# Three hand-written step lists of a fused recurrence and feed-forward kernel, replaced by three others

## The chip, the cores and the metric

One core of one Trainium2 chip. The metric is the device time of the whole program in microseconds: 584.02 us before, the median of three runs (581.95 to 585.95).

## The reference, cut to what matters

```
for t in range(S):                       # q, k, v, alpha: (4, 8, 768, 48)
    state = alpha[t][:, None] * state + outer(k[t], v[t])
    y[t] = q[t] @ state
x = y as (3072, 384)
h = x @ w_in                             # (384, 2048)
sp = max(h, 0) + log1p(exp(-abs(h)))     # softplus
out = (h * erf(sp)) @ w_out              # (2048, 384)
```

A gated linear recurrence over 768 positions in 32 streams, then a feed-forward layer over 3072 tokens. The weights come as 8-byte floats.

## The kernel before, in words

The recurrence is cut into 24 chunks, each of 64 positions of 16 streams (two batches). Two chunks give one block of 256 tokens for the feed-forward layer, so there are 12 blocks, numbered 0 to 11. The inner width 2048 is cut into four groups g, each group into two halves. Matrix products that need more precision than one pass are made of three: high times high, high times low, low times high.

All work is written as small steps, and three lists of step names give their order:

- `ld_n` loads a chunk (seven DMAs on SP's queue, L147 and L151; the buffers of alpha, k and q are single, so a load waits until the chunk before it has been read).
- `a1` to `a5` are the recurrence of a chunk. DVE: scan (L156), K (L169, L170, L175), Q (L178), masked scores (L203), state T (L253, L255), `x_lo` (L275). ACT: L164 to L166, `kn` (L191), `x_hi` (L274). PE: L187, L198, L226, L237. The second chunk's `a5` completes the x of a block.
- `wi_n` (12 of them) and `wo_n` (16) load one piece of a weight and split it in high and low: one DMA on SP's queue (L390), two operations on ACT (L396, L379), four on DVE (L398, L401, L404, L380). Group g of H needs wi_3g to wi_3g+2; O_g_half needs two pieces of wo. The staging tile of a wi comes from the pool of `hs`, that of a wo from the pool of `s`, and the work tile of both from the pool of `w`.
- `H_g_half` multiplies x by a half group of w_in (18 matmuls, L310) and copies it out on ACT (L315) into `hs`.
- `U_g` is a tanh on ACT (L321), `L1_g` two logarithms and an exponential on ACT (L326 to L328), `L2_g` two operations on DVE (L334, L335), `G_g` a gelu on ACT (L338), `Z_g` two operations on DVE (L342, L343).
- `O_g_half` splits a half group in high (`gh`: DVE L356 for O_0_0 and O_2_0, ACT L358 for the rest) and low (`gl`: DVE L359) and makes 12 matmuls (L367) into `acc`. `out` copies acc on ACT (L375) and stores it.
- `GELU` and `LN` load the table of functions on ACT (L115). U and G need the one, a2 and L1 the other, so a block passes U, LN, L1, GELU, G, Z, O.

A suffix @n means a block n further on, and numbers in the chunk steps count from the chunk that the list is given. Pools: 5 tiles for `s`, 7 for `hs`, 4 for `w`, two for `gh` and `gl`, two banks for `acc`, two for `ph`, one tile for `o`.

`START` runs once: it loads and splits the weights, and makes chunks 0 to 5, H to L2 of block 0 and six half groups of H of block 1. `ORDER` runs for i = 1 to 11: G to out of block i-1, the last two half groups of H, then U, L1 and L2 of block i, chunks 2i+4 and 2i+5, and six half groups of H of block i+1. `TAIL` runs once: G to out of block 11. The lists set priorities: the framework that builds the program takes, for each engine, the earliest step of the list whose inputs and buffers it reckons to be ready. Which order came out is read from the trace. A step whose block or chunk lies past the end is skipped.

Of the kernel before, what the change touches and what calls it, by code (L numbers as in the profile page):

```python
# [23 lines left out]
LNEXP, GELU = "natural_log_exp_and_others", "gelu_and_others"  # L24
# [2 lines left out]
START, ORDER, TAIL = (  # L27
    z.split()
    for z in (
# [10 lines left out]
    )  # L40
)

# [2 lines left out]
def gla_moe(ctx: ExitStack, tc: tile.TileContext, q, k, v, alpha, w_in, w_out, out):  # L45
# [10 lines left out]
    NBLK = NT // TB  # L56
# [30 lines left out]
    for i in range(NI):  # L87
        half = maskn[i * TC : (i + 1) * TC]
        nc.gpsimd.affine_select(
            out=half, in_=half, pattern=[[1, TC]], compare_op=ALU.is_ge, fill=0.0, base=0, channel_multiplier=-1  # L90
# [412 lines left out]
    def run(order, c0, b0):  # L503

        for step in order:
            name, _, rel = step.partition("@")
            name, *arg = name.split("_")
            arg = [int(z) for z in arg]
            if name == "wi":
                weight_in(*arg)  # L510
            elif name == "wo":
                weight_out(*arg)
            elif name[0] in "la":
                if c0 + arg[0] < len(chunks):
                    ch = chunks[c0 + arg[0]]
                    if name == "a5":
                        ch.a5(moes[ch.n // 2])
                    elif name == "a6":
                        pass
                    else:  # L520
                        getattr(ch, name)()
            elif name in TABLES:
                new_phase(TABLES[name])
            elif b0 + int(rel or 0) < NBLK:
                getattr(moes[b0 + int(rel or 0)], name)(*arg)

    run(START, 0, 0)
    for i in range(1, NBLK):
        run(ORDER, 2 * i + 4, i)
    run(TAIL, 2 * NBLK, NBLK - 1)  # L530

# [3 lines left out]
        out=top[:, 0:2], in_=flags.rearrange("p n two -> p two n"), op=ALU.max, axis=mybir.AxisListType.X  # L535
# [67 lines left out]
```

## Time and profile before

| | us |
|---|---|
| median of three runs | 584.02 |
| the profiled execution, its own time | 582.33 |
| its span, first to last instruction | 580.4 |
| PE busy in the span | 519.5 |
| DVE busy | 483.6 |
| ACT busy | 468.6 |

The mean granted clock of TensorE over the span is 0.969 of full. The profile gives busy times of the engines: PE multiplies, PEld loads its weights, DVE and ACT work elementwise, SP issues the DMAs. L-numbers are lines of the kernel before. In a timeline each row has a start, a duration, the engine, the line, what is written from what, and in brackets the idle time before it with what ended that time.

### The profile page before, as it was taken

How to read it: one execution, taken by the hardware profiler on the slowest of the kernel's cores; microseconds unless marked ns; L12 is line 12 of the kernel's file. 1: busy time of each engine (PE TensorE's matmuls, PEld its weight loads, DVE VectorE, ACT ScalarE, POOL GpSimd, SP SyncE). 2: the span in 40 equal slices, each digit the busy share in tenths (PEclk: the TensorE clock that was granted, in tenths of full speed). 3: DMA queues.
4: the chain of work that ended last, by engine and by line, in shares of the span. 5: the costliest groups of instructions: out<-in, count | busy, mean ns of one | idle time of the engine just before them, and what ended most of it. 6: DMA issues, size and time to landing. Idle time of an engine off the chain costs nothing.

```text
span 580.4 us, 16926 instructions
## 1 busy us (share of the span) xinstructions
PE 519.5 (90%) x7386; PEld 496.0 (85%) x7386; DVE 483.6 (83%) x688; ACT 468.6 (81%) x704; POOL 2.4 (0%) x16
## 2 busy tenths in 40 slices
PE   0588687499999999999999999999999999999584
PEld 0486686488989999999999999999999999999584
DVE  6779969999999979969789699699699698594970
ACT  4446799579999799699699798797896996989911
POOL 1000000000000000000000000000000000000000
PEclk9999799789999999999999999999999999999878
DMA  6575633522412222212202312221211100000000
GB/s 194 177 230 168 203 91 107 178 86 63 128 28 61 76 55 62 64 52 75 88 25 65 88 32 72 75 61 43 73 62 44 53 8 30 1 29 1 28 0 33
DMA packets 36370, 43.64 MB, mean 75 GB/s; under 512 B 21952, under 2 KB 25024, under 8 KB 36288
## 3 DMA queue, kind: packets, MB, share of 16 engines
q1 hardware_dynamic: 36288, 42.48, 24.3%
q8 instruction: 60, 0.98, 0.7%
q14 instruction: 22, 0.18, 0.1%
HBM read 37.75 MB, written 4.72 MB: 73 GB/s over the span
## 4 chain that ended last, share of the span: by engine, by line
PE 69%; DVE 15%; ACT 9%; issue 3%; DMA 2%; SPq 0%; ACTq 0%; DVEq 0%
PE acc L367 29%; PE ph L310 29%; PE py L226 4%; PE pS L198 3%; DVE wbuf L401 2%; DVE s L342 2%; ACT s L326 2%; PE pu L237 1%; PE pn L187 1%; DVE wbuf L404 1%; DVE A L156 1%; DVE t L334 1%; DVE w L335 1%; DVE hs L343 1%; ACT hs L315 1%
## 5 line engine op out<-in xcount | busy, mean ns | idle before, releaser
L310 PE MATMUL ph<-x_hi,wi_hi 128*128 128x256 f32 x576 | 166.9, 290 | 7.5 <-ACT wi_hi L379 4.8
L310 PE MATMUL ph<-x_lo,wi_hi 128*128 128x256 f32 x576 | 164.0, 285 | 0.0
L310 PE MATMUL ph<-x_hi,wi_lo 128*128 128x256 f32 x576 | 163.7, 285 | 0.3 <-DVE wi_lo L380 0.2
L367 PE MATMUL acc<-wo_hi,gh 128*128 128x384 f32 x384 | 133.2, 347 | 16.4 <-DVE gh L356 16.4
L367 PE MATMUL acc<-wo_hi,gl 128*128 128x384 f32 x384 | 131.4, 346 | 2.0 <-DVE gl L359 1.9
L367 PE MATMUL acc<-wo_lo,gh 128*128 128x384 f32 x384 | 131.0, 341 | 0.0
L310 PEld LDWEIGHTS ph<-x_hi,wi_hi 128*128 128x128 f32 x576 | 111.4, 194 | 10.1 <-ACT wi_hi L379 5.1
L359 DVE TENSOR_TENSOR gl<-hs,gh 128x512 fp32r<-128x512 f32 x96 | 64.9, 686 | 58.4 <-ACT gh L358 57.6
L310 PEld LDWEIGHTS ph<-x_hi,wi_lo 128*128 128x128 f32 x576 | 111.5, 194 | 1.0 <-DVE wi_lo L380 0.8
L310 PEld LDWEIGHTS ph<-x_lo,wi_hi 128*128 128x128 f32 x576 | 111.0, 193 | 0.5 <-DVE x_lo L275 0.3
L367 PEld LDWEIGHTS acc<-wo_hi,gh 128*128 128x128 f32 x384 | 73.8, 192 | 18.0 <-issue 8.7
L315 ACT ACTIVATE hs<-ph 128x512 f32<-128x512 f32 x96 | 56.3, 590 | 39.3 <-PE ph L310 38.1
L367 PEld LDWEIGHTS acc<-wo_hi,gl 128*128 128x128 f32 x384 | 72.7, 191 | 7.4 <-DVE gl L359 7.0
L367 PEld LDWEIGHTS acc<-wo_lo,gh 128*128 128x128 f32 x384 | 73.7, 192 | 0.0
L334 DVE TENSOR_TENSOR t<-s,w 128x1024 f32<-128x1024 f32 x48 | 58.5, 1218 | 1.9 <-ACT w L328 1.4
L335 DVE SCALAR_TENSOR_TENSOR w<-t,w 128x1024 f32<-128x1024 f32 x48 | 58.4, 1216 | 0.3
L358 ACT ACTIVATE gh<-hs 128x512 fp32r<-128x512 f32 x72 | 44.9, 625 | 16.3 <-PE acc L367 12.5
L343 DVE SCALAR_TENSOR_TENSOR hs<-s,hs 128x1024 f32<-128x1024 f32 x48 | 57.9, 1215 | 0.1
L342 DVE TENSOR_TENSOR s<-s,w 128x1024 f32<-128x1024 f32 x48 | 57.5, 1215 | 0.4 <-ACT s L338 0.4
L326 ACT ACTIVATE s<-s,fixed 128x1024 f32<-128x1024 f32 x48 | 54.6, 1141 | 0.0
L321 ACT ACTIVATE s<-hs 128x1024 f32<-128x1024 f32 x48 | 49.7, 1055 | 1.6 <-DVE wbuf L398 0.9
L328 ACT ACTIVATE w<-w 128x1024 f32<-128x1024 f32 x48 | 50.4, 1051 | 0.3
(62 smaller groups left out, 715.1 us busy)
## 6 DMA issues: line engine op xcount, KB each, us to landing
raw_v<-in_v_dram SPq DMA_DIRECT2D x24, 448.0 KB, 3.7
wst<-in_moe_w_in_dram SPq DMA_DIRECT2D x12, 512.0 KB, 5.7
wst<-in_moe_w_out_dram SPq DMA_DIRECT2D x16, 384.0 KB, 3.7
raw_a<-in_alpha_dram SPq DMA_DIRECT2D x48, 96.0 KB, 2.9
raw_k<-in_k_dram SPq DMA_DIRECT2D x48, 96.0 KB, 2.2
raw_q<-in_q_dram SPq DMA_DIRECT2D x48, 96.0 KB, 2.3
out_dram<-o SPq DMA_DIRECT2D x24, 192.0 KB, 1.9
```

The lines of the kernel that those rows point to most:

```text
L310: nc.tensor.matmul(out=o, lhsT=wt[:, kt, fs], rhs=xt[:, kt, :], start=n == 0, stop=n == 3 * KT - 1)
L315: nc.scalar.activation(self.hs[g][:, sl], ph, AF.Copy)
L321: tab(nc.scalar.activation(self.s[g], self.hs[g], AF.Tanh, scale=-0.5))
L326: tab(nc.scalar.activation(s, s, AF.Ln, scale=0.5 - 2.0**-24, bias=bhalf))
L328: tab(nc.scalar.activation(w, w, AF.Exp, scale=-1.0))
L334: nc.vector.tensor_tensor(out=t, in0=s, in1=w, op=ALU.mult)
L335: nc.vector.scalar_tensor_tensor(out=w, in0=t, scalar=2.0, in1=w, op0=ALU.add, op1=ALU.mult)
L342: nc.vector.tensor_tensor(out=s, in0=s, in1=w, op=ALU.mult)
L343: nc.vector.scalar_tensor_tensor(out=h, in0=s, scalar=RT2 / 2, in1=h, op0=ALU.subtract, op1=ALU.mult)
L358: nc.scalar.activation(ghf, gg, AF.Copy)
L359: nc.vector.tensor_tensor(out=gl.rearrange("p a t -> p (a t)"), in0=gg, in1=ghf.bitcast(F32), op=ALU.subtract)
L367: nc.tensor.matmul(out=self.acc[tt][:, :DM], lhsT=gt[:, u, ts], rhs=wt[:, f, :], start=f == 0 and n == 0, stop=f == NF - 1 and n == 2,)
```

## The change

The three lists are replaced, and the loop over `ORDER` is shortened by one pass at either end. The new `START` also holds what the first pass of `ORDER` had (G to out of block 0, the rest of block 1, chunks 6 and 7, six half groups of H of block 2). The new `ORDER` runs for i = 2 to 10. The new `TAIL` also holds what the last pass had (G to out of block 10, the rest of block 11). The number of steps of each kind, the instructions of a step and the tiles stay as they are, and the tables are loaded as often (26 times).

```diff
@@ -27,16 +27,21 @@
-        "wi_1 wi_3 ld_0 wi_0 a1_0 a2_0 a3_0 ld_1 a4_0 wi_2 wi_4 a1_1 a5_0 a2_1 a3_1 a4_1 ld_2 wi_6 a5_1 a1_2 "
-        "a2_2 wi_7 wi_5 H_0_0 H_0_1 a3_2 a4_2 H_1_0 ld_3 wo_0 H_1_1 a1_3 wi_8 a5_2 a2_3 GELU wi_10 a3_3 ld_4 "
-        "wi_9 H_2_0 wi_11 wo_1 H_2_1 a4_3 H_3_0 H_3_1 U_0 U_2 a5_3 wo_3 wo_2 U_1 U_3 a1_4 H_0_0@1 H_0_1@1 LN "
-        "wo_5 L1_0 a2_4 a3_4 H_1_0@1 H_1_1@1 wo_4 L1_1 ld_5 L1_2 H_2_0@1 L2_0 wo_7 L2_1 L1_3 L2_2 a1_5 a2_5 a3_5 "
-        "wo_15 L2_3 wo_10 a4_4 a5_4 wo_9 wo_8 wo_11 ld_6 H_2_1@1 a4_5 a5_5 wo_6 wo_14 wo_12 wo_13 ",
-        "GELU a1_0 G_0@-1 G_1@-1 Z_0@-1 H_3_0 G_2@-1 U_0 H_3_1 Z_1@-1 O_0_0@-1 U_2 O_0_1@-1 O_1_0@-1 G_3@-1 U_1 "
-        "Z_2@-1 O_2_1@-1 O_1_1@-1 U_3 LN Z_3@-1 O_2_0@-1 a2_0 L1_0 a3_0 L2_0 a4_0 H_0_0@1 ld_1 a5_0 a1_1 a2_1 "
-        "a3_1 O_3_0@-1 L1_1 H_1_0@1 ld_2 H_1_1@1 L2_1 L1_2 a4_1 O_3_1@-1 H_2_0@1 L1_3 L2_2 H_2_1@1 a5_1 H_0_1@1 "
-        "L2_3 out@-1 ",
-        "GELU G_0 Z_0 O_0_0 G_1 G_2 Z_1 G_3 O_1_1 O_0_1 Z_2 O_1_0 Z_3 O_2_0 O_2_1 O_3_0 O_3_1 out ",
+        "wi_1 wi_0 ld_0 wi_3 a1_0 a2_0 a3_0 ld_1 a4_0 wi_6 a1_1 wi_2 wi_7 a2_1 a5_0 a3_1 ld_2 a4_1 a1_2 wi_4 "
+        "wi_8 a2_2 a5_1 a3_2 wi_5 H_0_0 H_0_1 ld_3 H_1_0 a4_2 wo_0 H_1_1 a5_2 a1_3 wi_9 a2_3 a3_3 wi_10 H_2_0 "
+        "wi_11 H_2_1 wo_1 H_3_0 GELU H_3_1 U_0 a4_3 U_2 ld_4 wo_3 a5_3 a1_4 H_0_0@1 U_1 wo_2 wo_11 U_3 wo_4 "
+        "H_0_1@1 LN L1_0 a2_4 wo_5 a3_4 ld_5 L1_1 a4_4 L1_2 L2_0 L2_1 L2_2 wo_10 a1_5 wo_7 L1_3 H_2_0@1 a2_5 "
+        "H_1_0@1 wo_6 a5_4 H_2_1@1 a3_5 wo_9 L2_3 a4_5 wo_15 ld_6 H_1_1@1 wo_12 wo_14 GELU wo_13 a5_5 G_0 G_1 "
+        "Z_0 H_3_0@1 Z_1 a1_6 H_3_1@1 U_0@1 wo_8 O_0_0 G_2 U_3@1 O_0_1 U_2@1 G_3 Z_2 O_1_1 U_1@1 LN Z_3 O_1_0 "
+        "a2_6 O_2_1 a3_6 L1_0@1 H_0_0@2 L1_3@1 ld_7 L2_0@1 a4_6 a5_6 a1_7 a2_7 H_1_0@2 O_3_0 O_2_0 H_0_1@2 a3_7 "
+        "L2_3@1 a4_7 L1_2@1 H_2_0@2 O_3_1 H_1_1@2 L2_2@1 L1_1@1 out H_2_1@2 a5_7 L2_1@1 ld_8 ",
+        "GELU G_0@-1 G_3@-1 Z_0@-1 G_2@-1 Z_2@-1 G_1@-1 O_0_0@-1 H_3_0 H_3_1 U_2 O_0_1@-1 a1_0 Z_1@-1 U_0 "
+        "O_1_0@-1 U_1 U_3 H_1_0@1 LN Z_3@-1 O_2_0@-1 a2_0 a3_0 L1_0 O_1_1@-1 a4_0 ld_1 O_2_1@-1 H_0_0@1 L1_2 "
+        "a1_1 a5_0 H_2_0@1 a2_1 H_0_1@1 O_3_0@-1 a3_1 L2_2 a4_1 ld_2 L1_1 L1_3 O_3_1@-1 H_1_1@1 out@-1 L2_0 a5_1 "
+        "H_2_1@1 L2_3 L2_1 ",
+        "GELU H_3_0 G_0@-1 H_3_1 G_1@-1 G_2@-1 Z_2@-1 Z_0@-1 U_0 O_0_0@-1 G_3@-1 Z_1@-1 O_0_1@-1 U_2 O_2_1@-1 "
+        "U_1 U_3 LN O_1_0@-1 O_2_0@-1 O_1_1@-1 Z_3@-1 O_3_0@-1 L1_0 O_3_1@-1 L2_0 L1_1 L1_2 L1_3 L2_1 L2_3 GELU "
+        "G_0 L2_2 Z_0 O_0_0 G_2 G_3 O_0_1 G_1 Z_1 O_1_1 O_1_0 Z_2 Z_3 O_2_1 O_2_0 O_3_0 out@-1 O_3_1 out ",
@@ -525,7 +530,7 @@
     run(START, 0, 0)
-    for i in range(1, NBLK):
+    for i in range(2, NBLK - 1):
         run(ORDER, 2 * i + 4, i)
     run(TAIL, 2 * NBLK, NBLK - 1)
```

## Rows read from the trace of the kernel before

**Rows 1.** The page's part 1: busy time, share of the span, instructions.

```profile
PE 519.5 (90%) x7386; PEld 496.0 (85%) x7386; DVE 483.6 (83%) x688; ACT 468.6 (81%) x704; POOL 2.4 (0%) x16
```

**Rows 2.** Busy time of each engine by stage; the second number is the stage's length.

```profile
core 0: us, PE busy (x) PEld busy (x) DVE busy (x) ACT busy (x) POOL busy (x), PEclk, DMA share, GB/s
0.00:34.60 34.60, 12.48 (x328) 10.57 (x328) 24.74 (x43) 15.66 (x33) 2.41 (x16) 1.00 0.69 215
34.60:76.50 41.90, 34.70 (x557) 31.84 (x558) 36.48 (x72) 26.25 (x49) 0.00 (x0) 0.92 0.54 167
76.50:99.00 22.50, 17.40 (x305) 15.88 (x303) 18.24 (x30) 22.47 (x37) 0.00 (x0) 1.00 0.33 104
99.00:115.00 16.00, 8.29 (x214) 7.31 (x214) 15.94 (x29) 10.60 (x19) 0.00 (x0) 0.76 0.52 157
115.00:177.30 62.30, 60.01 (x710) 55.92 (x712) 61.21 (x93) 57.32 (x89) 0.00 (x0) 0.95 0.27 79
177.30:527.60 350.30, 350.30 (x5085) 339.82 (x5086) 297.94 (x392) 308.06 (x449) 0.00 (x0) 1.00 0.18 53
527.60:544.80 17.20, 17.20 (x100) 16.45 (x98) 10.61 (x13) 16.94 (x21) 0.00 (x0) 1.00 0.00 1
544.80:553.40 8.60, 0.06 (x2) 0.00 (x0) 8.20 (x10) 6.90 (x9) 0.00 (x0) 0.66 0.13 47
553.40:572.10 18.70, 18.62 (x95) 18.14 (x96) 10.23 (x13) 3.48 (x7) 0.00 (x0) 0.88 0.01 2
```

**Rows 3.** Chain that ended last: start, length, what; steady stage and end.

```profile
411.89 12.70 PE acc L367 x72
...
453.54 12.70 PE acc L367 x72
...
517.13 10.61 PE ph L310 x90
```

**Rows 4.** SP's queue in the first 45 us: issues of loads.

```profile
15.19 0.81 SPq L147 DMA_DIRECT2D raw_k<-in_k_dram  x2
...
17.44 0.91 SPq L390 DMA_DIRECT2D wst<-in_moe_w_in_dram  x2
...
28.01 1.40 SPq L390 DMA_DIRECT2D wst<-in_moe_w_in_dram  x3
```

**Rows 5.** Groups by line and shape: busy, mean ns, idle before.

```profile
L315 ACT ACTIVATE hs<-ph 128x512 f32<-128x512 f32 x96 | 56.3, 590 | 39.3 <-PE ph L310 38.1 <-DVE gl L359 1.0
...
L375 ACT ACTIVATE o<-acc 128x384 f32<-128x384 f32 x24 | 11.7, 488 | 8.1 <-DMA out_dram<-o 5.0 <-PE acc L367 3.2
...
L401 DVE SCALAR_TENSOR_TENSOR wbuf<-wbuf 128x384 int32<-128x384 int32 x16 | 8.8, 551 | 1.7 <-ACT wbuf L396 1.6
...
L401 DVE SCALAR_TENSOR_TENSOR wbuf<-wbuf 128x512 int32<-128x512 int32 x12 | 8.2, 687 | 1.5 <-ACT wbuf L396 1.2
...
L398 DVE TENSOR_SCALAR wbuf<-wst 128x384 int32<-128x384 int32 x16 | 5.6, 353 | 1.3 <-DMA wst<-in_moe_w_out_dram 1.3
```

**Rows 6.** DVE's timeline, first LN stage: a wo that came late.

```profile
80.40 0.56 DVE L401 SCALAR_TENSOR_TENSOR wbuf<-wbuf 128x384 int32<-128x384 int32 x1 [1.62 <-ACT wbuf L396]
```

**Rows 7.** DVE's timeline, 99 to 118 us: Z of block 0 and its first gl.

```profile
106.02 1.21 DVE L343 SCALAR_TENSOR_TENSOR hs<-s,hs 128x1024 f32<-128x1024 f32 x1
...
112.28 1.22 DVE L343 SCALAR_TENSOR_TENSOR hs<-s,hs 128x1024 f32<-128x1024 f32 x1
...
116.63 0.68 DVE L359 TENSOR_TENSOR gl<-hs,gh 128x512 fp32r<-128x512 f32 x1
```

**Rows 8.** DVE's timeline, steady stage: low parts of O_0_0 and O_0_1.

```profile
444.54 1.29 DVE L359 TENSOR_TENSOR gl<-hs,gh 128x512 fp32r<-128x512 f32 x2
```

**Rows 9.** DVE's timeline, after the last table load: Z of block 11.

```profile
548.19 2.51 DVE L342 TENSOR_TENSOR s<-s,w 128x1024 f32<-128x1024 f32 x2
550.62 2.35 DVE L343 SCALAR_TENSOR_TENSOR hs<-s,hs 128x1024 f32<-128x1024 f32 x2
552.89 0.42 DVE L356 CAST gh<-hs 128x512 fp32r<-128x512 f32 x1
```

## The prediction

> **What bounds the kernel now.** First read the busy times of the whole span: PE 90%, DVE 83%, ACT 81% [rows 1]. Such an average says little, since no instruction is added or taken away; what an order can change are the idle stretches of the engine that sets the pace. So next come the stages [rows 2]. From 177.3 to 527.6 us PE is busy for all of 350.3 us while DVE and ACT have a seventh of the time free: the middle is bound by PE. Before it, PE is not the bound. In 99 to 115 us it works 8.29 of 16 us, while DVE works 15.94; in 115 to 177.3 DVE works 61.21 of 62.3. In 76.5 to 99, the first LN stage, ACT is full (22.47 of 22.5). At the end PE stands still for 8.6 us (544.8 to 553.4), while DVE and ACT bring the last block through GELU, G and Z. The chain of waits says the same [rows 3]: in the middle it is matmuls alone, and one pass of the list lasts 453.54 - 411.89 = 41.65 us.
>
> So the time is a start, a middle that runs at PE's pace, and an end. Work that the start brings to PE earlier moves everything behind it. I make the sum on the profiled execution's own time of 582.33 us (its span and 1.9 us around it), which is 1.7 us below the median of 584.02.
>
> **The start.** All of DVE's work in the start (28 weight splits, the first chunks, L2 and Z) is the same after the change, and from 99 to 177.3 us DVE is full. So the start can only be shortened by filling DVE's idle time before that. It has 41.90 - 36.48 = 5.42 us in 34.6 to 76.5 and 22.50 - 18.24 = 4.26 us in 76.5 to 99 [rows 2], together 9.7 us. The earlier idle time, 34.6 - 24.74 = 9.9 us, is mostly the wait for the first loads and the first chunk's chain, which the new list starts with the same steps; I leave it alone.
>
> What can fill it is a weight that has landed. SP's queue is in order, and a chunk's load waits there until the chunk before has been read: k of chunk 1 goes out at 15.19, and the weights behind it only at 17.44; the next three leave at 28.01, behind chunk 2 [rows 4]. A moved ld takes its seven DMAs along, a moved weight one. Counted in the lists, the weights ahead of ld_2, ld_3 and ld_4 are 5, 8 and 11 in the old one and 6, 9 and 14 in the new. So one more weight is at hand from the start, three more by ld_4. Also, six pieces of wo are listed before the first LN, four in the old. In the LN stage a wo has one staging tile left (four of five `s` hold the block), and DVE waits for it, as in the 1.62 us at 80.40 [rows 6].
>
> A wo costs DVE 0.353 + 3 x 0.551 = 2.0 us, a wi some 0.4 + 3 x 0.687 = 2.5 us [rows 5]; DVE's two other operations of each are as long as L401. Two wo and one wi drawn into idle time are 4.0 + 2.5 = 6.5 us. Bounds: 0, if the waits for tiles and for ACT stay where they are; 9.7, if all idle time goes. On the bad side, the new list has two more wi ahead of a5_1, so the first H may come 2 x 2.5 = 5.0 us later; PE has 41.9 - 34.7 = 7.2 us idle just behind, which hides it. If that cover were gone, the start would be 5.0 us longer. I take -6.5 us, being two thirds of the way to the largest gain.
>
> Where it should show: Z_0 of block 0 is half done at 106.02, but other work holds the first low part until 116.63 [rows 7]; some four wo lie between, and two fewer would bring O_0_0 forward by about 4 us. What is late next is DVE itself, until PE has its backlog.
>
> **The middle.** Nine passes at PE's pace cost the same in any order so long as PE never waits: 0 us. The cover is this. In the old order PE ends H_3_1 of a block at 411.89 (where the O of the block before begins), and its first low parts stand from 444.54 + 0.7 = 445.2 on: a chain of 33.3 us through U, LN, four L1, GELU, G, Z. PE wants them at 453.54, so 8.3 us are spare [rows 3, 8]. In the new list O_0_0 of the block before stands ahead of H_3_0 and H_3_1. A half of O is 12.70 / 6 = 2.12 us and a half of H 10.61 / 5 = 2.12 us [rows 3], so the distance from H_3_1 to the next O_0_0 falls to 41.65 - 3 x 2.12 = 35.3 us, and the spare time to 2.0 us. As long as the chain stays at 33.3, the change costs nothing; below it is a rival.
>
> **The end.** After H_3_1 of block 11 PE has the eight halves of O of block 10 (17.2 us [rows 2]) and then waits for the chain. In both lists those halves stand behind H_3_1, so that wait stays. One thing moves: before, Z_0 and Z_1 run interleaved (two L342, two L343), and the first gh comes at 552.89 [rows 9]. The new list has L2_2, then Z_0 and O_0_0, then G_2. If Z_0 runs alone, two operations of 1.2 us go out of the way: -2.4 us. If L2_2 or another Z slips in, 0. On the bad side, out of block 10 stands behind most of the last block, and O_0_0 needs its acc; two copies of 0.49 us with the three gelus ahead of them (some 1.1 us each, an estimate: twice the 0.59 of a copy half as long [rows 5]) are about +4 us. I take half the gain, -1.2 us.
>
> The 96 matmuls of the last eight halves take 18.62 us against 8 x 2.12 = 17.0; the granted clock is 0.66 of full over the idle stretch, between the levels of 1.2 and 2.4 GHz, and 0.88 over the burst [rows 2]. The Trainium skill, "TensorE: Matmul & The Clock Gate", section "HAM oscillation — how this bites in real kernels", puts such a loss to the idle gap ahead of a burst, so that a shortened gap would not give it back. If the loss came instead from low parts that arrive late, it would go with the interleaving, and the sum would be 1.6 us lower, 573.0. The clock in the row speaks for the Trainium skill's reading, and the sum does not count the 1.6.
>
> **Sum.** 582.33 - 6.5 + 0 - 1.2 = 574.6; I say 575.
>
> **Rivals.**
> *More is won.* All 9.7 us go, the end gives 2.4, and PE's 62.3 - 60.0 = 2.3 us of idle time in the catching up as well: 582.3 - 14.4 = 568. For it: three more weights by ld_4. Against it: staging tiles limit how early a wo can be split.
>
> *Nothing that can be told.* The lists are only priorities. In the old list every wo stood ahead of Z_0, yet some four lay between its halves and the first low part [rows 7]: tiles, not the list, timed them. If tiles time them again, the start keeps its length, and the time is 580 to 584; I write 582. That is also what it would be if the order on the engines hardly changed.
>
> *Slower.* The middle loses its cover. Place: O_0_0 of each pass, PE waiting for gl. In the old LN stage ACT copies about one `hs`; the new list puts up to six H of the next block, and out, between LN and GELU. Five more copies at 0.59 and two of out at 0.49 [rows 5] are 3.9 us: 33.3 + 3.9 = 37.2 us against 35.3, so 1.9 us in each of nine passes, 17 us: 574.6 + 17 = 592. It decides from a chain of 35.3 us on, and makes the kernel slower by over 1% from 37.0 us. For it: ACT and DVE work in order, so a copy ahead of L1 holds it up. Against it: H's copies come as PE makes them, much of this ACT work lies in the idle time of either stage anyhow, and Z_0 now stands earlier than G_2.
>
> **Chances and range.** About 1% (5.8 us) is what a measurement of this kernel can tell from no change: faster means below 578.2, slower above 589.9. My forecast (571 to 578) 0.40, more won 0.16, nothing to be told 0.26, slower 0.18. So faster 0.56, same 0.26, slower 0.18. The range reaches from 564, somewhat under the case in which all idle time goes, to 592, the price of the slower case; what is left out is about 2 in 10. The likeliest case's own range is 568 to 578.
>
> **What would show it.** Right: O_0_0 of block 0 near 110 us instead of 115; DVE's idle time between 34 and 99 us down from 9.7 to about 3; PE full from some 171 us on; passes of 41.65 us; PE's last wait 6 to 8 us. Wrong: DVE's idle time where it was; PE waiting for gl once in each pass, with passes of 42 us or more; a wait for acc behind out in the end. If PE stays full in the middle and the total still moves by more than 10 us, the start did something that I have not seen.

## The result, and the profile after

The changed kernel takes 578.2 us (median of six runs, 577.48 to 578.48); the kernel before, in six runs beside it, 584.26 us (581.95 to 585.95). The ratio is 0.9898, 95% interval 0.9872 to 0.9925: some 6 us faster, and 3.2 us above the forecast. The profiled execution took 578.25 us. Line numbers of the kernel after are 5 higher (L310 is L315, L367 is L372, L359 is L364); in e1 to e3 below they are 21 higher than before, in e10 and e11 3.

Part 1 of the page after, for [rows 1]:

```profile
PE 517.6 (90%) x7386; PEld 497.2 (86%) x7386; DVE 484.6 (84%) x688; ACT 465.4 (81%) x704; POOL 2.4 (0%) x16
```

Counts are those of before, and busy times within 1%: what went is nearly all idle time. Busy time of each engine by stage after, cut at its own table loads, first O and last wait of PE (second number: length), for [rows 2]; the stretch from 521.9 begins 2.2 us ahead of the O of block 10, so its length isn't to be compared:

```profile
core 0: us, PE busy (x) PEld busy (x) DVE busy (x) ACT busy (x) POOL busy (x), PEclk, DMA share, GB/s
34.60:73.00 38.40, 34.27 (x571) 31.47 (x572) 34.73 (x68) 27.57 (x54) 0.00 (x0) 1.00 0.51 157
73.00:102.40 29.40, 22.74 (x353) 21.05 (x353) 25.22 (x43) 24.26 (x39) 0.00 (x0) 0.77 0.45 130
102.40:115.70 13.30, 4.86 (x158) 4.13 (x153) 13.09 (x23) 9.22 (x16) 0.00 (x0) 0.79 0.59 167
115.70:166.80 51.10, 49.39 (x655) 46.75 (x656) 50.81 (x75) 46.10 (x72) 0.00 (x0) 0.95 0.24 68
166.80:521.90 355.10, 355.10 (x5119) 346.33 (x5119) 301.35 (x398) 313.90 (x462) 0.00 (x0) 1.00 0.19 54
521.90:541.70 19.80, 19.68 (x119) 18.70 (x117) 13.59 (x17) 18.44 (x22) 0.00 (x0) 1.00 0.01 2
541.70:549.50 7.80, 0.00 (x0) 0.00 (x0) 7.41 (x8) 6.83 (x9) 0.00 (x0) 0.62 0.07 25
549.50:568.10 18.60, 18.50 (x94) 18.03 (x95) 12.34 (x15) 3.33 (x6) 0.00 (x0) 0.88 0.04 13
```

Read it against [rows 2] from the top. The first LN table comes at 73.0 instead of 76.5, and DVE's idle time up to the GELU table is 3.67 + 4.18 = 7.9 us, where it was 9.7. But the LN stage now lasts 29.4 us, not 22.5, and ACT, full in it before, is idle for 5.1 us. The stage also has a granted clock of 0.77 where it had 1.00: the half clock that before has ahead of it (0.92 in 34.6 to 76.5) is gone from there, and 13.65 us of it stand here from 82.8 on. The first O of block 0 begins at 115.7, where it began at 115.1. The last wait of PE begins at 541.7 instead of 544.8 and lasts 7.8 instead of 8.6 us.

The chain that ended last, after (start, length, what), for [rows 3]: the first rows of two passes, and the end.

```profile
328.61 4.17 PE acc L372 x24
...
369.91 4.17 PE acc L372 x24
...
542.06 1.24 DVE t L339
543.32 1.23 DVE w L340
544.54 1.14 DVE s L347
545.68 1.13 DVE t L339
546.81 1.14 DVE hs L348
547.95 0.06 DVE w L340
548.01 0.99 issue
549.00 0.43 DVE gh L361
```

The middle is matmuls alone, as before, with a pass of 369.91 - 328.61 = 41.30 us for 41.65. In the end one operation of L2 (L339) still stands between Z_0's two (L347, L348). A second one follows, which the chain shows only as "issue"; the timeline of DVE has it between Z_0 and `gh`:

```profile
547.87 1.22 DVE L340 SCALAR_TENSOR_TENSOR w<-t,w 128x1024 f32<-128x1024 f32 x1
```

Seen against this one execution of before, PE's last wait comes 3.1 us earlier. Nine passes of 0.35 us would make that up and leave nothing for the start, but the passes aren't alike: from one O_0_0 to the next they last 40.4 to 41.7 us before and 40.3 to 41.3 after. From the O_0_0 of block 2 to that of block 9 before takes 288.1 us and after 286.4, so 1.7 us lie there and some 1.4 ahead of it. Over the medians the gain is 6 us. So either the start did little or that execution of before was one of its better ones (before's six runs spread over 4 us, after's over 1). The first three runs were to say which.

### The profile page after: what moved, and what is told of

Its sections match the earlier page's. It is cut to its first block, busy times and chain, and to the rows that moved or that the text cites. A ratio compares the mean times of both kernels' runs of the same rounds, so it can differ in the third digit from the quotient of the medians.

```text
span 576.5 us, 16934 instructions
## 1 busy us (share of the span) xinstructions
PE 517.6 (90%) x7386; PEld 497.2 (86%) x7386; DVE 484.6 (84%) x688; ACT 465.4 (81%) x704; POOL 2.4 (0%) x16
## 4 chain that ended last, share of the span: by engine, by line
PE 75%; DVE 11%; ACT 8%; issue 3%; DMA 3%; ACTq 0%; DVEq 0%
PE ph L315 31%; PE acc L372 31%; PE py L231 5%; PE pS L203 4%; PE pu L242 2%; PE pn L192 2%; DVE wbuf L406 1%; DVE t L339 1%; DMA wst<-in_moe_w_out_dram 1%; DVE A L161 1%; ACT w L332 1%; ACT s L331 1%; DVE wbuf L409 1%; ACT hs L320 1%; ACT w L333 1%
## 5 line engine op out<-in xcount | busy, mean ns | idle before, releaser
L315 PE MATMUL ph<-x_hi,wi_hi 128*128 128x256 f32 x576 | 165.6, 288 | 3.8 <-ACT x_hi L279 2.5
L315 PE MATMUL ph<-x_hi,wi_lo 128*128 128x256 f32 x576 | 163.0, 284 | 0.9 <-DVE wi_lo L385 0.9
L315 PE MATMUL ph<-x_lo,wi_hi 128*128 128x256 f32 x576 | 163.0, 283 | 0.1
L372 PE MATMUL acc<-wo_hi,gh 128*128 128x384 f32 x384 | 133.0, 346 | 15.5 <-DVE gh L361 15.5
L372 PE MATMUL acc<-wo_hi,gl 128*128 128x384 f32 x384 | 130.3, 342 | 1.8 <-DVE gl L364 1.5
L372 PE MATMUL acc<-wo_lo,gh 128*128 128x384 f32 x384 | 130.6, 340 | 0.0
L315 PEld LDWEIGHTS ph<-x_hi,wi_hi 128*128 128x128 f32 x576 | 110.2, 192 | 5.7 <-ACT x_hi L279 2.6
L315 PEld LDWEIGHTS ph<-x_hi,wi_lo 128*128 128x128 f32 x576 | 111.2, 194 | 1.5 <-DVE wi_lo L385 1.4
L315 PEld LDWEIGHTS ph<-x_lo,wi_hi 128*128 128x128 f32 x576 | 110.5, 192 | 0.4 <-DVE x_lo L280 0.4
L372 PEld LDWEIGHTS acc<-wo_hi,gh 128*128 128x128 f32 x384 | 73.5, 191 | 17.3 <-ACT o L380 8.2
L364 DVE TENSOR_TENSOR gl<-hs,gh 128x512 fp32r<-128x512 f32 x96 | 65.0, 686 | 27.6 <-ACT gh L363 26.5
L372 PEld LDWEIGHTS acc<-wo_hi,gl 128*128 128x128 f32 x384 | 72.7, 191 | 4.0 <-DVE gl L364 4.0
L372 PEld LDWEIGHTS acc<-wo_lo,gh 128*128 128x128 f32 x384 | 73.4, 191 | 0.0
L339 DVE TENSOR_TENSOR t<-s,w 128x1024 f32<-128x1024 f32 x48 | 58.6, 1221 | 6.4 <-ACT w L333 6.1
L348 DVE SCALAR_TENSOR_TENSOR hs<-s,hs 128x1024 f32<-128x1024 f32 x48 | 58.4, 1219 | 0.0
L347 DVE TENSOR_TENSOR s<-s,w 128x1024 f32<-128x1024 f32 x48 | 57.8, 1217 | 0.0
```

What stands on the lines that cost most here:

```text
L315: nc.tensor.matmul(out=o, lhsT=wt[:, kt, fs], rhs=xt[:, kt, :], start=n == 0, stop=n == 3 * KT - 1)
L339: nc.vector.tensor_tensor(out=t, in0=s, in1=w, op=ALU.mult)
L347: nc.vector.tensor_tensor(out=s, in0=s, in1=w, op=ALU.mult)
L348: nc.vector.scalar_tensor_tensor(out=h, in0=s, scalar=RT2 / 2, in1=h, op0=ALU.subtract, op1=ALU.mult)
L364: nc.vector.tensor_tensor(out=gl.rearrange("p a t -> p (a t)"), in0=gg, in1=ghf.bitcast(F32), op=ALU.subtract)
L372: nc.tensor.matmul(out=self.acc[tt][:, :DM], lhsT=gt[:, u, ts], rhs=wt[:, f, :], start=f == 0 and n == 0, stop=f == NF - 1 and n == 2,)
```

## The experiments

**The three parts alone.** Each kernel takes one list of the new ones and keeps the old ones for the rest.

```diff
 e1_start_only:  new START; old ORDER for i = 2 to 11; old TAIL
 e2_order_only:  old START; old ORDER for i = 1; new ORDER for i = 2 to 10; old ORDER for i = 11; old TAIL
 e3_tail_only:   old START; old ORDER for i = 1 to 10; new TAIL
```

> The new START with the old ORDER (i = 2 to 11) and the old TAIL. Theory A (the prediction: the start gives most) expects 4 to 6.5 us less than before, near 578 to 580. Theory B (from the trace after: the first LN stage is longer by 7 us and takes back what came earlier, O_0_0 of block 0 starts at 115.7 as against 115.1) expects 0 to 1.5 us less, near 583 to 584. Passes stay at 41.65 us.

> The old START, the old ORDER for i = 1 and 11, the new ORDER for i = 2 to 10, the old TAIL. Theory A expects no change (PE is full in the middle). Theory B (a pass of the new order lasts 41.30 us instead of 41.65 at the same PE work) expects 9 x 0.34 = 3 us less, near 581.

> The old START, the old ORDER for i = 1 to 10, the new TAIL. Both theories expect 0.7 to 1.2 us less, near 583: PE's last wait 7.9 us instead of 8.6. If Z_0 really ran alone, it would be 2.4 us less.

| run | us | ratio to before | 95% |
|---|---|---|---|
| e1_start_only | 580.24 | 0.994 | 0.9915 to 0.9964 |
| e2_order_only | 583.42 | 0.9986 | 0.9963 to 1.0009 |
| e3_tail_only | 583.58 | 0.9991 | 0.9969 to 1.0014 |

The start is most of it (-3.6 us); the other two cannot be told from nothing by their times. Their traces say more: e2's longest passes are 41.31 us, as after, and those of e1 and e3, which have the old ORDER, 41.43. From the O_0_0 of block 2 to that of block 9, seven passes, e2 takes 286.6 us, e1 287.7 and e3 287.5. So the new order is worth about 1 us. (Three passes of before's profile last 41.65, 0.2 us longer still; why isn't settled.) PE's last wait is 8.60 us in e1 and e2 and 7.87 in e3: the tail is worth 0.7 us. With 3.6 for the start that is 5.3 of the 6 us.

Where START gains in this profile can be read off as well, since e1 has before's middle and end. O_0_0 of blocks 0, 1 and 2 begins at 114.25, 162.12 and 203.54 in e1; in before at 115.09, 162.11 and 205.63. So 2.1 us go in the pass from block 1 to block 2, where before's PE waits 1.1 us for a low part and e1's doesn't; the rest of them wasn't traced. The timeline of PE in before:

```profile
163.73 0.44 PE L367 MATMUL acc<-wo_hi,gl 128*128 128x384 f32 x1 [1.11 <-DVE gl L359]
```

Where the 0.12 us lie can be read in e1's trace. The timeline of PE in e1 (start, duration, line; successive matmuls of O):

```profile
413.35 0.34 PE L388 MATMUL acc<-wo_hi,gh 128*128 128x384 f32 x1
413.52 0.34 PE L388 MATMUL acc<-wo_lo,gh 128*128 128x384 f32 x1
413.80 0.44 PE L388 MATMUL acc<-wo_hi,gl 128*128 128x384 f32 x1
414.08 0.34 PE L388 MATMUL acc<-wo_hi,gh 128*128 128x384 f32 x1
```

The usual step from start to start is 0.17 us; two here are 0.28, around a matmul with `gl`. The timeline of DVE in e1 shows this `gl` just in time, made from 413.05 to 413.74, behind a `gh` that ACT makes late:

```profile
413.05 0.69 DVE L380 TENSOR_TENSOR gl<-hs,gh 128x512 fp32r<-128x512 f32 x1 [3.53 <-ACT gh L379]
```

That is a wait too short to be named in the waits; the pair stands once in each old pass and in no new one. It is the third half of O, whose `gh` comes on ACT behind a tanh and the LN table (411.10), and not O_0_0, whose cover of 8.3 us I had counted. The pair costs 0.22 us and these passes differ by 0.12, so the new order loses a tenth elsewhere; where wasn't traced.

**More weights early, alone.** Before's list, with the wi pieces drawn forward and nothing else.

```diff
-a2_2 wi_7 wi_5 H_0_0 H_0_1 a3_2 a4_2 H_1_0 ld_3 wo_0 H_1_1 a1_3 wi_8 a5_2 a2_3 GELU wi_10 a3_3 ld_4 wi_9 H_2_0 wi_11 wo_1
+a2_2 wi_7 wi_8 wi_5 H_0_0 H_0_1 a3_2 a4_2 H_1_0 ld_3 wi_9 wi_10 wo_0 H_1_1 a1_3 a5_2 a2_3 GELU wi_11 a3_3 ld_4 H_2_0 wo_1
```

> The kernel before with wi_8 to wi_11 listed earlier in START and nothing else moved. Theory B now says that the new START wins because PE no longer waits some 4 us for wi_hi in the H of block 0 (66.8 to 69.7 us in three profiles of the old START) and does not run part of that stage at half clock (6.8 to 13.6 us of it). It expects that wait below 1 us, the first LN table at 72 to 75 us, and 2 to 4 us less than before, near 580 to 582, with less spread. Theory C, that the gain of START comes from the places of the wo and of the steps behind the first LN, expects no change from before, 583.8.

It took 586.12 us (ratio 1.0043, 1.002 to 1.0067): slower. The 4.2 us wait for wi_hi fell to 1.83 us at the most, but TensorE was still at half clock from 67.1 to 73.9, and PE got a new wait of 4.59 us at 131.7 for `gh` from ACT. In all it has 10.2 us at half clock before 80 us, and its LN table comes at 76.29, no earlier than in before. So the state that theory B speaks of did not come about, and the run doesn't decide it; it shows that pieces of weight moved forward by themselves push something else back.

**Which part of START.** The new list up to its first LN with the old steps behind it, and the other way round; ORDER and TAIL old.

```diff
 e10_prefix_new:  new START up to its first LN, then the steps still missing in the old order
 e11_suffix_new:  old START up to its LN, then the steps still missing in the new order
```

> The new START up to its first LN, then the remaining steps of the old START and of the first pass of ORDER in their old order; old ORDER and TAIL. Theory E expects the gain of START here: first LN table at 72 to 74 us, and 2.5 to 4 us less than before, near 580 to 581.5. Theory C expects at most 1 us less.

> The old START up to its first LN, then the new START's steps behind its LN (wo_11 and wo_4, which the new one lists earlier, first); old ORDER and TAIL. Theory E expects no gain beyond 1 to 1.5 us and the spread of before (4 to 5 us), since the waits for wi_hi stay. Theory C expects the whole gain of START, 3 to 4 us.

e10 took 580.85 us (0.9952, 0.9931 to 0.9974), e11 586.95 us (1.007, 1.0042 to 1.0097). So the part ahead of LN by itself brings most of the gain (-2.8 against e1's -3.6), and the part behind it by itself costs 3 us on the old front. The two don't add up: on the new front the part behind LN costs nothing (e1 against e10). It is not that the first O comes early: in e10 it begins at 115.15, after PE waited 10.21 us for it. The O_0_0 of block 1 does, at 160.61 for before's 162.11, but e10 still has the wait for `gl` behind it (1.02 us at 162.15), which the new steps behind LN take away.

The waits of PE between 60 and 80 us (what it waits for; total, times, longest), in e11 and then in the kernel after:

```profile
PE ph L313 <- ACT wi_hi L382: 4.2, 1, 4.2
```

```profile
PE ph L315 <- ACT wi_hi L384: 0.9, 1, 0.9
```

Before it is 4.2 us as well, and a stretch at half clock begins at its end. The same window view around it, in before, in e3 and e2 (old front both) and after; the number behind POOL is the granted clock:

```profile
66.00:73.00 7.00, 6.02 (x26) 5.73 (x27) 6.97 (x15) 4.72 (x9) 0.00 (x0) 0.52 0.25 71
```

```profile
57.00:62.00 5.00, 4.59 (x37) 4.01 (x38) 5.00 (x9) 1.84 (x4) 0.00 (x0) 0.66 0.89 321
68.00:75.00 7.00, 6.07 (x27) 5.77 (x28) 6.97 (x15) 4.71 (x9) 0.00 (x0) 0.51 0.10 33
```

```profile
57.00:64.00 7.00, 7.00 (x73) 6.13 (x75) 4.96 (x8) 2.26 (x6) 0.00 (x0) 0.52 0.80 282
70.00:77.00 7.00, 6.33 (x31) 6.12 (x30) 6.97 (x14) 3.99 (x7) 0.00 (x0) 0.54 0.01 2
```

```profile
66.00:73.00 7.00, 6.57 (x58) 6.55 (x56) 6.82 (x17) 6.25 (x12) 0.00 (x0) 1.00 0.37 102
```

In the 7 us around the wait PE is busy for over 6 in all of them, but the kernel after makes 58 matmuls where before makes 26. With the old front, these three executions have 6.8, 10.2 and 13.6 us at 1.2 GHz before 80 us, their first O at 115.1, 117.3 and 119.9, and their times are 582.33, 583.59 and 585.49 (e3 and e2 lose 0.7 and 1 us less behind it).

The profiles of e8 and e11, old front too, have 6.8, and each is the fastest run of its kernel. The runs of before go the same way: of the 62 beside e1 to e11 (one, at 607.36 us, far off the rest) the 35 with a mean granted clock of 0.966 or more have a median of 582.0 us, the 15 with 0.961 or less one of 585.7. With the new front (after, e1, e4, e6, e7, e10) the clock is full from 41 to 80 us. So before's profiled execution was one of the better ones, and the start's gain is read wrongly off it. But the half clock isn't gone with the new front: after, e1, e4, e6 and e7 have 13.65 us of it from 81 to 83 us on, in the LN stage, beside a wait of PE of some 6 us, and there PE has idle time left (22.74 of 29.4 us busy).

**Is it the half clock or the wait?** 52 matmuls that nobody reads were put into the waits of before, 16 behind H_1_1 and 36 ahead of H_2_0.

```diff
-H_1_0 ld_3 wo_0 H_1_1 a1_3 wi_8 a5_2 a2_3 GELU wi_10 a3_3 ld_4 wi_9 H_2_0
+H_1_0 ld_3 wo_0 H_1_1 D_16 a1_3 wi_8 a5_2 a2_3 GELU wi_10 a3_3 ld_4 wi_9 D_36 H_2_0
```

> The kernel before with 52 extra matmuls of block 0's x that nobody reads (16 behind H_1_1, 36 ahead of H_2_0), to fill PE's two waits in the H of block 0. It adds 6.1 us of PE work at full clock and takes nothing away. Theory E: the runs of before spread over 581 to 586 because after these waits PE runs 6.8 to 13.6 us of this stage at half clock (three profiles: 6.8, 10.2 and 13.6 us with 582.3, 583.6 and 585.5 us), and the new START has no such wait. It expects less half clock between 40 and 80 us, the first LN table by 75 us, and a median 1.5 to 2.5 us below before, near 581.5 to 582.5, though PE does more. Theory C (the half clock there does not reach the end) expects before or 1 to 4 us more.

It took 596.39 us (1.0223, 1.0188 to 1.0258), and it decides nothing. Only 3.4 us at half clock were left before 80 us, yet PE still waits there (0.94 and 3.2 us), LN came at 77.24 and the first O at 117.46. And losses of another kind came with the added work; the waits of PE over the whole span of this kernel:

```profile
PE pu L237 <- issue: 7.0, 4, 2.2
PE py L226 <- issue: 3.2, 1, 3.2
```

"Issue" is idle time in which PE waited for nothing that the profile shows. The four at L237 lie in passes of the middle (203.95, 371.57, 416.78, 461.70), far behind the added matmuls. What the half clock costs by itself stays open.

**Why the first O did not move.** The timeline of ACT after, in the first LN stage (idle time before and what ended it in brackets):

```profile
86.61 1.14 ACT L331 ACTIVATE s<-s,fixed 128x1024 f32<-128x1024 f32 x1
...
98.80 0.52 ACT L384 ACTIVATE wo_hi<-wbuf 128x384 fp32r<-128x384 f32 x1
99.94 1.06 ACT L332 ACTIVATE w<-s 128x1024 f32<-128x1024 f32 x1 [0.62 <-DVE wo_lo L385]
...
102.45 1.28 ACT L120 ACT_TABLE_LOAD   x1
```

The fourth L1 makes its first logarithm at 86.61 and its second at 99.94, when a piece of wo has been split: the second one needs a tile of the pool `w`, which has four, and the new list has wo_10 and wo_7 ahead of L1_3. So the GELU table waits. It is the same in e11, where the second logarithm runs at 103.58, the table comes at 106.08 and the first O at 119.08. Two kernels test it: e4 moves L1_3 alone, e6 also lists nine pieces of wo behind Z_0 (its expectation says ten).

```diff
 e4_l1_3_early, against the kernel after
-L1_2 L2_0 L2_1 L2_2 wo_10 a1_5 wo_7 L1_3 H_2_0@1
+L1_2 L1_3 L2_0 L2_1 L2_2 wo_10 a1_5 wo_7 H_2_0@1
 e6_wo_behind, against e4
-L2_2 wo_10 a1_5 wo_7 H_2_0@1 a2_5 H_1_0@1 wo_6 a5_4 H_2_1@1 a3_5 wo_9 L2_3 a4_5 wo_15 ld_6 H_1_1@1 wo_12 wo_14 GELU wo_13 a5_5
+L2_2 a1_5 H_2_0@1 a2_5 H_1_0@1 a5_4 H_2_1@1 a3_5 L2_3 a4_5 ld_6 H_1_1@1 GELU a5_5
-G_0 G_1 Z_0 H_3_0@1 Z_1 a1_6 H_3_1@1 U_0@1 wo_8 O_0_0 G_2 U_3@1 O_0_1 U_2@1 G_3 Z_2 O_1_1 U_1@1 LN Z_3
+G_0 G_1 Z_0 O_0_0 H_3_0@1 Z_1 O_0_1 wo_6 wo_7 a1_6 H_3_1@1 U_0@1 wo_10 G_2 wo_12 U_3@1 wo_13 U_2@1 G_3 Z_2 O_1_1 wo_14 wo_15 U_1@1 LN wo_9 wo_8 Z_3
```

> The kernel after, with L1_3 of block 0 listed right behind L1_2, ahead of wo_10 and wo_7 (one step moved). Theory B says that in the first LN stage L1_3 waits for its w tile, which a piece of wo holds (its second logarithm runs at 99.94, its first at 86.61): with L1_3 first, the GELU table should come at 95 to 98 us instead of 102.5 and O_0_0 of block 0 at 108 to 112 instead of 115.7; the time then falls by 2 to 5 us below the kernel after, if DVE does not lose it again on the pieces of wo that now come later. Theory A, for which the tile does not matter, expects the same time as after, 578.

> The kernel after with L1_3 of block 0 early and with ten pieces of wo listed behind Z_0 or later. If the place of the wo in the list holds up Z_0 and the first O (theory B), the first O of block 0 starts at 104 to 110 us instead of 115, and the time is 2 to 5 us below the kernel after, unless O_1 and later halves then wait for their wo. If the work of DVE as a whole sets the end of the start (theory D), PE's first O is earlier but PE then waits more between 110 and 165 us, and the time is within 1.5 us of the kernel after.

> The kernel after once more, to stand beside e5 and e6 on one chip: 577.5 to 578.5, 1.0% below before.

| run | us | ratio to before | 95% | GELU table | first O |
|---|---|---|---|---|---|
| after | 578.2 | 0.9898 | 0.9872 to 0.9925 | 102.45 | 115.73 |
| e7_after_again (beside e6) | 577.31 | 0.9896 | 0.9864 to 0.9929 | | 115.44 |
| e4_l1_3_early | 577.35 | 0.989 | 0.9864 to 0.9917 | 95.29 | 114.76 |
| e6_wo_behind | 574.95 | 0.9862 | 0.9828 to 0.9895 | 96.54 | 106.67 |

e4 shows the tile: with L1_3 ahead of the wo the table comes 7.2 us earlier. But the first O gains 1 us, and the time nothing that can be told. So the tile alone does not hold up the first O. The timeline of DVE in e4 says why:

```profile
103.55 1.22 DVE L348 SCALAR_TENSOR_TENSOR hs<-s,hs 128x1024 f32<-128x1024 f32 x1
104.69 0.55 DVE L385 TENSOR_TENSOR wo_lo<-wbuf,wo_hi 128x384 fp32r<-128x384 f32 x1
...
108.50 0.55 DVE L385 TENSOR_TENSOR wo_lo<-wbuf,wo_hi 128x384 fp32r<-128x384 f32 x1
...
110.47 0.55 DVE L385 TENSOR_TENSOR wo_lo<-wbuf,wo_hi 128x384 fp32r<-128x384 f32 x1
...
112.14 0.55 DVE L385 TENSOR_TENSOR wo_lo<-wbuf,wo_hi 128x384 fp32r<-128x384 f32 x1
...
114.28 0.42 DVE L361 CAST gh<-hs 128x512 fp32r<-128x512 f32 x1
```

The Z of two groups are done at 104.8, and four pieces of wo with parts of two more, some of whose loads have only just landed, stand in DVE's order ahead of `gh`. With them behind Z, in e6:

```profile
103.12 2.35 DVE L348 SCALAR_TENSOR_TENSOR hs<-s,hs 128x1024 f32<-128x1024 f32 x2
105.39 0.42 DVE L361 CAST gh<-hs 128x512 fp32r<-128x512 f32 x1
```

The first O begins 9 us earlier than after. Of these 9 us, 2.4 come out at the end (e7 beside it: 577.31 - 574.95; five of e6's six runs lie below all of e7's). The windows of e6 show where the rest went:

```profile
106.70:160.00 53.30, 47.38 (x646) 44.35 (x645) 52.92 (x90) 46.83 (x75) 0.00 (x0) 0.97 0.36 113
```

DVE works 52.92 of these 53.3 us, and PE stands still for 5.9 of them in waits for low parts, copies and the wo that were put off. The wo have to be split before O can use them, wherever the list puts them. e6 is 9 us below before and the fastest version of this study.

**A shorter cover in the middle.** To test whether it is the place of H_3_1 that makes the short stalls, before's ORDER with H_3_1 behind O_0_1.

```diff
-H_3_0 G_2@-1 U_0 H_3_1 Z_1@-1 O_0_0@-1 U_2 O_0_1@-1 O_1_0@-1
+H_3_0 G_2@-1 U_0 Z_1@-1 O_0_0@-1 U_2 O_0_1@-1 H_3_1 O_1_0@-1
```

> The kernel before with one step of ORDER moved: H_3_1 behind O_0_1 of the block before, as the new ORDER also puts H between the first O. Theory B (in the old order PE runs out of prepared low parts while ACT makes U_3 and the LN table, and stands some 0.1 us twice in each pass) expects these two steps gone from the trace and passes of 41.2 to 41.3 us instead of 41.4, about 1 to 2 us in all, hardly more than the interval. If instead the chain from H_3_1 to O_0_0 becomes the bound, as my slower rival had it, passes grow above 41.7.

It took 587.78 us (1.0086, 1.0053 to 1.0119). The steps of 0.28 us are still there (419.69, 419.96), behind a `gl` that again waits for ACT's `gh` (made from 418.94 to 419.63), and a pass lasts 41.50 us, so H_3_1's place alone is not what the new order gains by. The loss is in the end; the timeline of PE in e8:

```profile
543.77 0.44 PE L367 MATMUL acc<-wo_hi,gh 128*128 128x384 f32 x1 [1.89 <-ACT gh L358]
...
545.42 0.62 PE L367 MATMUL acc<-wo_hi,gl 128*128 128x384 f32 x2 [0.69 <-DVE gl L359]
...
555.82 0.66 PE L367 MATMUL acc<-wo_hi,gh 128*128 128x384 f32 x1 [8.74 <-DVE gh L356]
```

PE waits 1.89 + 0.69 + 8.74 = 11.3 us there instead of 8.6, since the last O of block 10 stand closer to the chain that feeds them. Those 2.7 us are what this profile is longer than before's (585.02 to 582.33); it is e8's fastest run, and what the others lose beside it wasn't traced.

## Why the prediction was partly right

**The start was mis-sized, and its way was wrong.** The term was -6.5 us; the new START alone measured -3.6. The step that failed is "two fewer would bring O_0_0 forward by about 4 us": the first O came 0.6 us later. I also misread the rows behind it: the operation at 106.02 ends Z_0 and the one at 112.28 is Z_1's [rows 7], so Z_0 was not half but wholly done at 107.2. The timeline of DVE after has for these rows:

```profile
109.16 1.22 DVE L348 SCALAR_TENSOR_TENSOR hs<-s,hs 128x1024 f32<-128x1024 f32 x1
...
116.80 0.68 DVE L364 TENSOR_TENSOR gl<-hs,gh 128x512 fp32r<-128x512 f32 x1
```

There are indeed fewer wo between the end of Z_0 and the first low part: 9 of their DVE operations after, 15 before, four to a wo. But the end of Z_0 itself comes 3.1 us later, because the first LN, 3.5 us earlier, is followed by an L1_3 that waits 12 us between its logarithms for a tile held by wo; and where that tile is free (e4), wo in DVE's order still hold `gh`. I counted how early a wo can be taken up, and not whose tile it holds meanwhile or whom it keeps waiting on DVE.

The rival "nothing that can be told" had this half right: the first O stood within 0.6 us of where it was, though not by tiles alone. It missed the part ahead of LN, where the new list takes the 4.2 us wait for wi_hi away and the half clock out of that stage (e10), whatever the price of either, and the wait of 1.1 us for `gl` at 163.73 (e1). That START gave over half of its term by these other ways, none of which the sum had, was luck.

**Idle time of DVE.** It fell from 9.7 to 7.9 us, not to 3. And e6, whose first O is early, shows that bringing the first O forward by 9 us is worth 2.4: the cost of the weight work is mostly moved and not taken away. No version here came to the bound of -9.7; e6, less some 1.7 us for order and tail, is about 7 us below before.

**The baseline.** I made the sum on the profiled execution because it lay only 1.7 us below the median. The spread of 4 us in three runs of before was on the table, and I did not ask what varied. The old front varies by more: before's runs spread over 5.1 us (26 runs), those of e1 and e10 over 2.7 and 2.8, the twelve of after and e7 over 2.2. That the half clock behind the waits makes the difference is argued from the profiles and not shown alone. Of the 6 us between the medians some 2 are of this kind (the profiles differ by 4.1), and no step of the sum had them.

**The middle was right in its mechanism.** PE sets the pace in both, and the chain from H_3_1 to O_0_0 fitted into the shorter distance. After, H_3_1 of a block ends where O begins at 411.06, and O_0_0 of that block begins at 446.04, 35.0 us later; the timeline of DVE has the low parts between them:

```profile
443.66 1.29 DVE L364 TENSOR_TENSOR gl<-hs,gh 128x512 fp32r<-128x512 f32 x2
```

The first of the two stands by 444.4, so the chain is 33.3 us, as forecast. No steady pass has a wait for `gl`, and the slower rival's 37.0 us did not come. The 0 missed about 1 us in all, which the waits did not show and only the steps between matmuls do.

**The end was right in sign, by luck.** -0.7 us against -1.2. Z_1 did go out of the way, but two operations of L2 slipped in for it, one between Z_0's two and one behind them, which is the case that the sum put at 0. Six operations of 1.2 us stand in PE's wait in either kernel, for 7.10 us before (545.79 to 552.89) and 6.94 after (542.06 to 549.00). The rest is where they begin: 0.9 us behind the start of PE's wait before, 0.4 after. The first two before, ahead of those in [rows 9]:

```profile
545.79 1.23 DVE L334 TENSOR_TENSOR t<-s,w 128x1024 f32<-128x1024 f32 x1 [0.30 <-ACT w L328]
547.05 1.23 DVE L335 SCALAR_TENSOR_TENSOR w<-t,w 128x1024 f32<-128x1024 f32 x1
```

There was no wait for `acc` behind out. The burst of the last 96 matmuls takes 18.50 us at a granted clock of 0.88, where it took 18.62 [rows 2], so the 1.6 us were not given back, and the forecast did well to leave them out. By the reading of the Trainium skill, "TensorE: Matmul & The Clock Gate", section "HAM oscillation — how this bites in real kernels", that loss belongs to the idle gap ahead, and the trace agrees: a gap of 7.8 us is still there, and PE is busy for 18.50 of the 18.60 us behind it, with no wait for low parts among them.

**What would have shown it.** PE's last wait of 6 to 8 us came (7.87); PE full from 171 on came earlier (its last gap of over 0.3 us in the catching up is at 140.26). O_0_0 near 110 did not come, and DVE's 3 us did not.

## What to carry to other kernels

A place in a list does not only set when a step runs but how long it holds a tile that the critical chain wants: before bulk work is drawn into an idle stretch, list who else takes tiles from its pool. Bulk work listed ahead of the first consumer delays it in that engine's order (here by 8 to 9 us), and put behind it, most of that comes back as waits later (2.4 us were kept), so only the difference counts. And where the runs of a kernel spread by more than the gain that is sought, one profile of it is no baseline: take several, and compare the stretch that differs between them.

## What was not expected of the hardware

- With the same instructions ahead, executions of one front differ in how much of the first 80 us is at 1.2 GHz: 6.8, 10.2 and 13.6 us in three profiles, each stretch beginning within a microsecond or so of the end of a wait of PE of 2 to 4 us. The runs of before, whose time goes with their mean granted clock, spread over 5 us; how much of that the half clock itself makes isn't shown.
- A matmul whose low part was done only 0.06 us ahead of it shows as two steps of 0.28 instead of 0.17 us, with no idle time in the waits; the new order has no such pair.
- With 52 unused matmuls in the waits, idle times of 1.5 to 2.2 us called "issue" stood up to hundreds of us later, and the time was 12.8 us longer. Why isn't known.
